# A gated linear attention and a SiLU feed-forward block on one core: weight conversion regrouped, GpSimd's arithmetic moved, activation tables shared, and the order of all engines written out

## The chip, the core and the metric

The kernel runs on one core of a Trainium2 chip. A core has five engines that run side by side, each through its own instructions in order: TensorE (PE in the profile; its weight loads are shown apart as PEld), VectorE (DVE), ScalarE (ACT), GpSimd (POOL) and SyncE (SP), which only starts transfers. The metric is the time of one execution in microseconds on the device. Three runs of the kernel before gave 823.57, 825.14 and 825.61 us, median 825.14.

## The reference

For each of 4 batches and 8 heads (768 steps, head size 48) a complex state is carried along the sequence and read out; the result goes through a feed-forward block with SiLU:

```python
scale = np.minimum(mag, 0.999) / (mag + 1e-06)          # mag = |a_re + i a_im|
a_re_n, a_im_n = (a_re * scale, a_im * scale)
for t in range(S):
    new_re = ar * S_re - ai * S_im
    new_im = ar * S_im + ai * S_re
    kv = np.einsum('bhd,bhe->bhde', k[:, :, t], v[:, :, t])
    S_re, S_im = (new_re + kv, new_im)
    y[:, :, t] = np.einsum('bhd,bhde->bhe', q[:, :, t], S_re)
...
h = x @ w_in                                            # x: 3072 x 384, w_in: 384 x 2048
g = h * (1.0 / (1.0 + np.exp(-h)))
return (g @ w_out).astype(np.float32)                   # w_out: 2048 x 384
```

q, k, v and the gates are float32. The two weight matrices arrive as float64.

## The kernel before

The sequence is cut into chunks of 128 steps. A block n is one chunk of one batch with all 8 heads: 24 blocks, taken as 12 pairs p. Per pair the work is:

- **Gates.** `gates_log` (lines 203 to 235) and `gates_angle` (237 to 250) turn a_re and a_im into the logarithm of the capped magnitude (tile `l`) and the angle in turns (tile `th`), both 128 x 768 for a pair. ACT does squares, Ln, Exp and arctangent, DVE and POOL the arithmetic between them: POOL adds and multiplies `mag` (L227, L231).
- **Phases and sums.** `phases` (264) and `sums` (285) are matmuls with a triangle of ones, which make running sums of `th` and `l` over the chunk. `carried` (255) adds the last angle of the block one chunk earlier, by a transfer of one row and an addition on POOL (L262).
- **Rotation.** `trig` (279) takes sine and cosine, `decays` (297) the exponentials of the running sums, `rotated` (309) multiplies k and q by both (on POOL, L314, and DVE, L318), `turned` (322) transposes them: for blocks 0 to 3 (`EARLY`) on PE with a copy by ACT, later by DVE in pieces of 32 x 32 (L339) and 12 transfers (L344).
- **Attention.** `weights` (347) makes q times k and masks it (L356), `state` (391) updates the carried state (L404, and L405 on POOL), `output` (359) makes the attention's result, already transposed, as tile `xT`, the feed-forward's input. A third of its rows goes through a small tile `y3` and six transfers (L389).
- **Feed-forward.** `hidden` (411) makes 256 of the 2048 hidden columns for a pair (6 matmuls 128 x 256), a tanh on ACT and one operation on DVE (L420); `result` (424) multiplies them into the output, 4 matmuls 128 x 384. A pair has 8 of each; I call one such piece an h group or an r group.

The weights are converted from float64 once, as they arrive, by `load_w` (125 to 156), in 28 units: 12 of w1 (128 x 512) and 16 of w2 (128 x 384). Each unit is loaded as pairs of 32-bit words; ACT squares the upper word (L143), DVE joins the words in five operations (L144 to L152), and a sixth (L154) sets weights under the float32 range to zero, with the square as the test. An h or r group of pair 0 or 1 cannot run before the units it reads.

The program has a set-up part (lines 569 to 657), in which pairs 0 and 1 go through the feed-forward beside the conversion and pairs 0 to 2 through the attention, and ten steps p = 3 to 12 (`step`, 461), which run the feed-forward of pair p - 1, the attention of pair p and the gates of pairs p + 1 and p + 2. Only PE's order is that of the program text (`manual_schedule` with PE alone); the order on the other engines is chosen by a scheduler at build time, except that table loads and table functions on ACT are chained in text order. ACT must load a table (L186) when it changes between groups of functions.

A last part checks the smallest decay, and only if it is too small would a slow form of the whole computation (`step_by_step`) run; with these inputs it does not.

Of the kernel before, what the change touches and what calls it, by code (L numbers as in the profile page):

```python
# [17 lines left out]
LN_CAP = math.log(0.999)  # L18
# [9 lines left out]
L_MIN = -60.0  # L28


@with_exitstack
def kernel(
# [36 lines left out]
    EARLY = 4  # L69
# [6 lines left out]
    moe = fast.enter_context(tc.tile_pool(name="moe", bufs=2))  # L76
    p_m = fast.enter_context(tc.tile_pool(name="p_m", bufs=2, space=PSUM))
    p_h = fast.enter_context(tc.tile_pool(name="p_h", bufs=2, space=PSUM))
    p_o = fast.enter_context(tc.tile_pool(name="p_o", bufs=4, space=PSUM))
# [12 lines left out]


    def load_a(p):
        for name, ap in (("re", a_re), ("im", a_im)):
            A[p][name] = pre.tile([C, 2, H, D], F32, tag=name, name=f"{name}{p}", bufs=2)
            for i in range(2):
                b, c = place(2 * p + i)
                nc.sync.dma_start(
                    out=A[p][name][:, i], in_=ap[b].rearrange("h (c p) d -> p c h d", p=C)[:, c])  # L100

    def load_x(n, queue=None):
        b, c = place(n)
        for name, ap in (("k", k), ("q", q), ("v", v)):
            X[n][name] = ld.tile([C, H, D], F32, tag=name, name=f"{name}{n}",
                                 bufs=4 if name == "v" else 2)
            (queue or nc.sync).dma_start(
                out=X[n][name], in_=ap[b].rearrange("h (c p) d -> p c h d", p=C)[:, c])

    w1 = consts.tile([C, ND, DF], F32)  # L110
    w2 = consts.tile([C, NJ, DM], F32)

    def load_w1(cols, dc):


        last = (H - 2) * D
        third = D // ND
        rows = [(0, 2 * dc * D, D), (D, last + third * dc, third),
                (64, (2 * dc + 1) * D, D), (64 + D, last + D + third * dc, third)]
        load_w(w1[:, dc, ts(cols, WC)], [(at, w_in[r:r + n, ts(cols, WC)]) for at, r, n in rows])  # L120
# [4 lines left out]
    def load_w(dst, parts):  # L125

# [5 lines left out]
        raw = moe.tile([C, WC, 2], I32, tag="raw", name="raw", bufs=3)[:, 0:n]  # L134
        for at, src in parts:
# [3 lines left out]
        t = dst.bitcast(I32)  # L139
        u = moe.tile([C, WC], I32, tag="wu", name="u", bufs=1)[:, 0:n]  # L140
        x = moe.tile([C, WC], F32, tag="wx", name="x", bufs=1)[:, 0:n]

        nc.scalar.activation(out=x, in_=hi.bitcast(F32), func=AF.Square)  # L143
        nc.vector.tensor_scalar(out=t, in0=hi, scalar1=3, scalar2=0x3FFFFFF8,  # L144
                                op0=ALU.logical_shift_left, op1=ALU.bitwise_and)
        nc.vector.scalar_tensor_tensor(out=t, in0=hi, scalar=-0x40000000, in1=t,
                                       op0=ALU.bitwise_and, op1=ALU.bitwise_or)
        nc.vector.tensor_scalar(out=u, in0=t, scalar1=-0x800000, scalar2=None,
                                op0=ALU.bitwise_and)
        nc.vector.scalar_tensor_tensor(out=u.bitcast(F32), in0=lo, scalar=2.0 ** -52,  # L150
                                       in1=u.bitcast(F32), op0=ALU.mult, op1=ALU.mult)
        nc.vector.tensor_tensor(out=dst, in0=dst, in1=u.bitcast(F32), op=ALU.add)  # L152

        nc.vector.scalar_tensor_tensor(out=dst, in0=x, scalar=1.265625 * 2.0 ** -30, in1=dst, op0=ALU.is_ge,  # L154
                                       op1=ALU.mult)
# [10 lines left out]

    one_b = consts.tile([C, 1], F32)
    nc.gpsimd.memset(one_b, 1.0)
    half_pi_b = consts.tile([C, 1], F32)
    nc.gpsimd.memset(half_pi_b, math.pi / 2)  # L170
    ident = consts.tile([C, C], F32)
# [5 lines left out]
    chained = []  # L177

    def chain(ins):
        if chained:  # L180
# [4 lines left out]
    def table(name):  # L185
        chain(nc.scalar.preload_act_table_set(name))  # L186
# [5 lines left out]
    def flat(t):  # L192
# [612 lines left out]
```

## Time and profile before

| | |
|---|---|
| median of three runs | 825.14 us |
| the profiled execution | 825.82 us |
| its span, first to last instruction | 824.0 us |
| mean granted clock of TensorE | 0.92 |
| DVE busy | 430.0 us (52%) |
| ACT busy | 300.4 us (36%) |
| POOL busy | 131.8 us (16%) |

The page of the profile gives the busy time of each engine, the same in 40 equal slices of the span, the costliest groups of instructions with the idle time before them and what ended it, and the chain of work that ended last. The trace can also be asked for the busy time in any stretch, for the instructions of an engine in order of time, and for what each engine waited for. A group's row reads: line, engine, operation, output <- inputs, shape, count | busy us, mean ns of one | idle us before, and what ended it. The granted clock is the share of TensorE's full speed that it was allowed.

### The profile page before, as it was taken

The numbers are of one execution on the slowest core, as the hardware profiler recorded it, in microseconds if no ns is written. First come the engines' busy times: TensorE is split into PE (matmuls) and PEld (weight loads), VectorE is DVE, ScalarE is ACT, GpSimd is POOL, SyncE is SP. The second block draws the span as 40 slices with busy tenths as digits, with TensorE's granted clock in tenths as the row PEclk, the third lists the DMA queues.
The fourth block names the chain that finished last, engine by engine and source line by source line (L and its number), as shares of the span: only waits on it lengthen the run. The fifth ranks groups of instructions, "written<-read, shape, count | busy, mean of one in ns | idle before, by whom it ended". The sixth has DMA issues, their size and how long they took to land.

```text
span 824.0 us, 9608 instructions
## 1 busy us (share of the span) xinstructions
PE 701.7 (85%) x3488; PEld 524.2 (64%) x3488; DVE 430.0 (52%) x622; ACT 300.4 (36%) x470; POOL 131.8 (16%) x108
## 2 busy tenths in 40 slices
PE   0586468908896599999999999899999899999997
PEld 0365345605574486777777877677768677777774
DVE  2858858796556635653663565526436613521110
ACT  4655522451135441541543624515515411411111
POOL 0020210140005103230240231121212400200000
PEclk9768779867897699999999999899999899999999
DMA  9613645425513533524415434434344142230000
GB/s 175 118 39 85 121 126 115 96 65 127 96 30 73 91 54 54 114 34 89 78 20 102 76 48 85 76 43 88 62 77 79 25 86 49 31 68 9 20 0 24
DMA packets 281943, 58.68 MB, mean 71 GB/s; under 512 B 274056, under 2 KB 278304, under 8 KB 281888
## 3 DMA queue, kind: packets, MB, share of 16 engines
q1 hardware_dynamic: 275648, 56.80, 37.4%
q10 hardware_dynamic: 6240, 1.18, 1.1%
q8 instruction: 30, 0.49, 0.2%
q14 instruction: 25, 0.20, 0.1%
HBM read 36.25 MB, written 4.76 MB: 50 GB/s over the span
## 4 chain that ended last, share of the span: by engine, by line
PE 60%; DVE 13%; issue 12%; ACT 7%; DMA 2%; POOL 2%; SPq 2%; ACTq 1%; DVEq 0%; POOLq 0%
PE o L430 25%; PE h L416 23%; PE a L352 3%; PE y L372 2%; PE s L399 2%; PE y L375 2%; DVE sq L339 2%; ACT L186 2%; PE L L291 2%; ACT mag L189 1%; DVE qr L318 1%; PE phase L270 1%; ACT cs L189 1%; POOL mag L227 1%; DMA raw<-in_moe_w_in_dram 1%
## 5 line engine op out<-in xcount | busy, mean ns | idle before, releaser
L430 PE MATMUL o<-w,g 128*128 128x384 f32 x768 | 275.5, 507 | 48.0 <-DVE w L154 47.3
L416 PE MATMUL h<-xT,w 128*128 128x256 f32 x1152 | 271.5, 387 | 3.9 <-DMA xT<-y 2.3
L416 PEld LDWEIGHTS h<-xT,w 128*128 128x128 f32 x1152 | 221.7, 194 | 55.9 <-issue 7.9
L430 PEld LDWEIGHTS o<-w,g 128*128 128x128 f32 x768 | 148.7, 197 | 143.5 <-DVE w L154 54.1
L420 DVE SCALAR_TENSOR_TENSOR g<-g,h 128x512 f32<-128x512 f32 x96 | 65.5, 682 | 276.3 <-ACT g L189 276.0
L189 ACT ACTIVATE g<-h 128x512 f32<-128x512 f32 x96 | 57.2, 597 | 312.9 <-PE h L416 312.9
L352 PE MATMUL a<-T 96*128 96x128 f32 x384 | 52.1, 292 | 14.3 <-DMA T<-sq 9.1
L352 PEld LDWEIGHTS a<-T 96*128 96x128 f32 x384 | 50.5, 207 | 18.3 <-DVE re L245 9.5
L186 ACT ACT_TABLE_LOAD x45 | 57.7, 1283 | 10.5 <-issue 9.7
L405 POOL TENSOR_TENSOR S<-S,decs 96x384 f32<-96x384 f32 x16 | 14.8, 925 | 238.3 <-DVE S L404 211.4
L227 POOL TENSOR_TENSOR mag<-mag,s 128x768 f32<-128x768 f32 x11 | 26.0, 2363 | 153.9 <-DVE s L199 108.5
L318 DVE TENSOR_TENSOR kr<-L,cs 128x768 f32<-128x768 f32 x24 | 41.9, 1769 | 14.4 <-POOL L L314 14.3
L270 PE MATMUL phase<-th,upto 128*128 128x384 f32 x48 | 21.4, 572 | 27.9 <-DVE th L249 23.2
L372 PE MATMUL y<-w,v 128*64 128x128 f32 (+1 forms) x384 | 42.6, 300 | 1.4 <-DVE w L356 1.2
L314 POOL TENSOR_TENSOR L<-k,L 128x384 f32<-128x384 f32 x20 | 20.9, 1061 | 129.6 <-ACT L L189 102.0
L399 PEld LDWEIGHTS s<-v,kr 128*96 128x96 f32 x320 | 33.4, 182 | 11.3 <-DVE w L356 7.4
L399 PE MATMUL s<-v,kr 128*96 128x48 f32 x320 | 33.8, 264 | 6.0 <-DVE w L356 6.0
L189 ACT ACTIVATE mag<-mag 128x768 f32<-128x768 f32 (+1 forms) x39 | 30.5, 789 | 23.1 <-POOL mag L227 21.0
L356 DVE TENSOR_TENSOR w<-a,upto 128x512 f32<-128x512 f32 x48 | 31.7, 683 | 12.9 <-PE a L352 12.8
L375 PE MATMUL y<-T,S 96*64 96x128 f32 x320 | 36.3, 287 | 0.0
L143 ACT ACTIVATE x<-raw 128x384 f32<-128x384 f32 (+1 forms) x28 | 17.0, 606 | 48.8 <-DVE w L154 45.0
L381 ACT COPY xT<-y 128x384 f32<-128x384 f32 x24 | 11.4, 473 | 57.6 <-PE y L375 39.3
(63 smaller groups left out, 641.6 us busy)
## 6 DMA issues: line engine op xcount, KB each, us to landing
T<-sq SPq DMA_DIRECT2D x240, 64.0 KB
raw<-in_moe_w_out_dram SPq DMA_DIRECT2D x16, 384.0 KB
re<-in_a_re_dram SPq DMA_DIRECT2D x24, 192.0 KB
im<-in_a_im_dram SPq DMA_DIRECT2D x24, 192.0 KB
raw<-in_moe_w_in_dram SPq DMA_DIRECT2D x24, 192.0 KB
out_dram<-ot SPq DMA_DIRECT2D x24, 192.0 KB
v<-in_v_dram SPq DMA_DIRECT2D x22, 192.0 KB
k<-in_k_dram SPq DMA_DIRECT2D x22, 192.0 KB
```

The lines of the kernel that those rows point to most:

```text
L186: chain(nc.scalar.preload_act_table_set(name))
L189: chain(nc.scalar.activation(out=out, in_=in_, func=func, **kw))
L227: lambda s1=s1, mag=mag: helper.tensor_tensor(out=mag, in0=mag, in1=s1, op=ALU.add),
L318: nc.vector.tensor_tensor(out=x[w + "r"], in0=heads(e).unsqueeze(2).to_broadcast([C, H, 2, D]), in1=x["cs"], op=ALU.mult)
L352: nc.tensor.matmul(ps[:, h], lhsT=x["kT"][:, hh * HH + h], rhs=x["qT"][:, hh * HH + h], start=True, stop=True)
L356: nc.vector.tensor_tensor(out=x["w", hh], in0=ps, in1=upto.unsqueeze(1).to_broadcast([C, HH, C]), op=ALU.mult)
L372: nc.tensor.matmul(to, lhsT=v_[:, cols], rhs=x["w", h // HH][:, h % HH], start=True, stop=not carried)
L375: nc.tensor.matmul(to, lhsT=x["S"].rearrange("p h d -> p (h d)")[:, cols], rhs=x["qT"][:, h], start=False, stop=True)
L399: nc.tensor.matmul(ps[:, h], lhsT=x["kr"][:, h].rearrange("p c d -> p (c d)"), rhs=x["v"][:, h], start=True, stop=True)
L416: nc.tensor.matmul(ps[:, ji], lhsT=w1[:, dc, ts(jp * 2 + ji, C)], rhs=A[p]["xT"][:, dc], start=(dc == 0), stop=(dc == ND - 1))
L420: nc.vector.scalar_tensor_tensor(out=g, in0=g, scalar=1.0, in1=ps, op0=ALU.add, op1=ALU.mult)
L430: nc.tensor.matmul(A[p]["o"][m], lhsT=A[p]["g", jp][:, ji, ts(m, C)], rhs=w2[:, j], start=(j == 0), stop=(j == NJ - 1))
```

## The change

- **Conversion.** The sixth operation per unit (L154) is gone. ACT does two passes per unit in place of one: a square scaled up, and a Relu whose sum goes to a column of a new tile `tiny`, which is above zero only if some weight is under the float32 range. The last check then also looks at `tiny`, and the slow form, which would convert again with the mask, runs in that case too. The units are ordered in four rounds of 3 units of w1 and 4 of w2; each round feeds two h and two r groups of both pairs, which PE takes together. Five buffers for arriving words in place of three.
- **GpSimd.** None of its arithmetic is left: `mag`, `rotated`, `state` and `carried` do it on DVE. In its place POOL starts transfers: in the set-up the loads of a_re, a_im of pairs 1 to 4, of q, k, v of pairs 1 to 3, and the six transfers of `y3`; throughout, those of `decs`. The results leave through ACT's queue (L479 after).
- **Gates.** Absolute values move from DVE to ACT; the factor 0.5 of `l` goes into the matrix of ones (`half`), which saves DVE an operation per pair.
- **Tables.** Tanh is taken from the table that also has arctangent or sine, so there are three loads in a step of the loop.
- **Transposes.** Blocks 4 to 7 are also transposed on PE (`EARLY = 8`), through the two buffers of `p_m`.
- **Order.** In the ten steps every engine's order is that of the text, and the text is a list of names (`usual`, and `first` for p = 3). The PSUM space of the set-up is given to a third buffer for h and one for phases and sums; the squares of a pair's gates are made a step earlier.

```diff
-    EARLY = 4
+    EARLY = 8
...
-        raw = moe.tile([C, WC, 2], I32, tag="raw", name="raw", bufs=3)[:, 0:n]
+        raw = su.tile([C, WC, 2], I32, tag="raw", name="raw", bufs=5)[:, 0:n]
...
-        nc.scalar.activation(out=x, in_=hi.bitcast(F32), func=AF.Square)
...
-        nc.vector.scalar_tensor_tensor(out=dst, in0=x, scalar=1.265625 * 2.0 ** -30, in1=dst, op0=ALU.is_ge,
-                                       op1=ALU.mult)
+        joined(nc, dst, lo, hi, u)
+        x = su.tile([C, WC], F32, tag="wx", name="x", bufs=1)[:, 0:n]
+        nc.scalar.activation(out=x, in_=hi.bitcast(F32), func=AF.Square, scale=2.0 ** 15)
+        nc.scalar.activation(out=x, in_=x, func=AF.Relu, scale=-1.0, bias=least_b,
+                             accum_out=tiny[:, ds(len(units), 1)])
...
-            (nc.vector if n < EARLY else nc.gpsimd).tensor_tensor(
+            nc.vector.tensor_tensor(
                 out=e, in0=x[w].rearrange("p h d -> p (h d)"), in1=e, op=ALU.mult)
...
-                nc.sync.dma_start(out=xT[64 * r + D:64 * r + 64, dc],
-                                  in_=y3[64 * r + third * dc:64 * r + third * (dc + 1)])
+                (nc.sync if late else nc.gpsimd).dma_start(
+                    out=xT[64 * r + D:64 * r + 64, dc],
+                    in_=y3[64 * r + third * dc:64 * r + third * (dc + 1)])
...
-            nc.gpsimd.tensor_tensor(out=new, in0=new, in1=by, op=ALU.mult)
+            nc.vector.tensor_tensor(out=new, in0=new, in1=by, op=ALU.mult)
...
-        ps = p_h.tile([C, 2, T], F32, tag="h", name=f"h{p}_{jp}")
+        pool = late[2] if late and jp % 3 == 2 else p_h
+        ps = pool.tile([C, 2, T], F32, tag="h", name=f"h{p}_{jp}")
...
-    conv = [(1, s, lambda s=s, dc=dc: load_w1(s, dc)) for s in range(2) for dc in range(ND)]
+    conv = []
     for s in range(4):
+        conv += [(1, s, lambda s=s, dc=dc: load_w1(s, dc)) for dc in range(ND)]
         conv += [(2, j // 2, lambda j=j: load_w2(j)) for j in range(4 * s, 4 * s + 4)]
-        if s < 2:
-            conv += [(1, s + 2, lambda s=s, dc=dc: load_w1(s + 2, dc)) for dc in range(ND)]
...
+        groups("r0 r0 r1 r1 h1 h1")
...
+    usual = ("c h h E kA qA L F h kB h tA G r qB r h tB r th h A X r h r aA pA sA yA h pB aB S r lA "
+             "sB yB r lB D r")
+    first = ("c h h E kA qA L F h kB h G r qB r h th r tA h A tB X r h r aA pA sA yA h pB aB S r lA "
+             "sB yB r lB D r")
+    by_hand.append(True)
+    with tc.manual_schedule():
         for p in range(3, NP + 1):
-            step(p, parts(hidden, p - 1), parts(result, p - 1))
+            step(p, parts(hidden, p - 1), parts(result, p - 1), first if p == 3 else usual)
```

In the list h and r are groups of the feed-forward; E are the decays, k, q and t the rotation and transposes of a block, a, s and y its weights, state and output, p and l its phases and sums, S sine and cosine, L, F, G, th and D parts of the gates, c, A and X loads; A and B behind a letter name the two blocks of the pair.

Three places of the order. The first is VectorE in the set-up, before; `raw` is an arriving unit, `w_79` is w1 and `w_80` w2, `u` and `x` the two helper tiles, `g` the result of a tanh.

```order
L144 TENSOR_SCALAR w_79<-raw 128x512
L146 SCALAR_TENSOR_TENSOR w_79<-raw,w_79 128x512
L148 TENSOR_SCALAR u<-w_79 128x512
L150 SCALAR_TENSOR_TENSOR u<-raw,u 128x512
L152 TENSOR_TENSOR w_79<-w_79,u 128x512
L154 SCALAR_TENSOR_TENSOR w_79<-x,w_79 128x512
L420 SCALAR_TENSOR_TENSOR g_0_793<-g_0_793,h_0_786 128x512
```

The same engine in the set-up of the change, where w1 is `w_84`:

```order
L45 TENSOR_SCALAR w_84<-raw 128x512
L47 SCALAR_TENSOR_TENSOR w_84<-raw,w_84 128x512
L49 TENSOR_SCALAR u<-w_84 128x512
L50 SCALAR_TENSOR_TENSOR u<-raw,u 128x512
L52 TENSOR_TENSOR w_84<-w_84,u 128x512
L462 SCALAR_TENSOR_TENSOR g_2_798<-g_2_798,h_2_791 128x512
```

The multiplication by the mask, which came last and waited for ACT's square, is gone; the unit is ready one operation earlier.

The second place is TensorE in the set-up, before, from the sums of pair 2 on; `xT_369` and `xT_584` are the inputs of pairs 0 and 1, `o_0_694` and `o_0_816` their outputs.

```order
L291 MATMUL L_868<-l_704,upto 128x384
L416 MATMUL h_2_897<-xT_584,w_79 128x256 x6
L430 MATMUL o_0_694<-w_80,g_2_779 128x384 x2
L430 MATMUL o_1_695<-w_80,g_2_779 128x384 x2
L416 MATMUL h_3_922<-xT_584,w_79 128x256 x6
L430 MATMUL o_0_694<-w_80,g_3_813 128x384 x2
L430 MATMUL o_1_695<-w_80,g_3_813 128x384 x2
L430 MATMUL o_0_816<-w_80,g_2_904 128x384 x2
L430 MATMUL o_1_817<-w_80,g_2_904 128x384 x2
L416 MATMUL h_4_1048<-xT_369,w_79 128x256 x6
```

TensorE at the same place of the change; here pairs 0 and 1 have `xT_385` and `xT_649`, and pair 2's angles are `th_835`.

```order
L457 MATMUL h_2_956<-xT_649,w_84 128x256 x6
L457 MATMUL h_3_966<-xT_649,w_84 128x256 x6
L457 MATMUL h_4_986<-xT_385,w_84 128x256 x6
L457 MATMUL h_5_996<-xT_385,w_84 128x256 x6
L306 MATMUL phase_1006<-th_835,upto 128x384
L306 MATMUL phase_1011<-th_835,upto 128x384
L327 MATMUL L_1016<-l_834,half 128x384
L327 MATMUL L_1020<-l_834,half 128x384
L472 MATMUL o_0_946<-w_85,g_2_963 128x384 x2
L472 MATMUL o_1_947<-w_85,g_2_963 128x384 x2
```

Groups now come in twos per pair, and the r groups stand further behind the h groups whose results they read, and behind the conversions.

The third place is GpSimd in the set-up, before, after its constants: its work on pairs 1 to 3.

```order
L227 TENSOR_TENSOR mag_267<-mag_267,s_265 128x768
L231 TENSOR_TENSOR mag_267<-mag_267,im_115 128x768
L227 TENSOR_TENSOR mag_703<-mag_703,s_701 128x768
L231 TENSOR_TENSOR mag_703<-mag_703,im_292 128x768
L262 TENSOR_TENSOR th_720<-th_720,carry_725 1x384
L262 TENSOR_TENSOR th_720<-th_720,carry_728 1x384
L227 TENSOR_TENSOR mag_989<-mag_989,s_987 128x768
L231 TENSOR_TENSOR mag_989<-mag_989,im_735 128x768
```

GpSimd of the change, the end of the loads that stand ahead of the first of the six transfers of `y3` (`y_0_387`) into pair 0's `xT_385`:

```order
L145 DMA v_344<-in_v_dram 128x8x48
L134 DMA im_1025<-in_a_im_dram 128x8x48
L134 DMA im_1025<-in_a_im_dram 128x8x48
L145 DMA v_557<-in_v_dram 128x8x48
L134 DMA re_1024<-in_a_re_dram 128x8x48
L134 DMA re_1024<-in_a_re_dram 128x8x48
L145 DMA v_563<-in_v_dram 128x8x48
L428 DMA xT_385<-y_0_387 16x256
```

The engine's arithmetic is replaced by transfers that it starts, 24 of them ahead of the one that the first h group needs.

More of the change, by code (lines that the diff above doesn't have):

```diff
@@ L565, in turns, with groups @@
         both(trig, p)
-        table("exp_and_others")
+        table("exp")
         both(decays, p)
+    def groups(order):
+        for x in order.split():
+            (h if x[0] == "h" else r)(int(x[1]))
+    g = nc.gpsimd
     with tc.manual_schedule(engines={mybir.EngineType.PE}):
-        angles(0, True)
+        load_a(1, g)
+        gates(0, True)
+        table("trig")
+        gates_atan(0, True)
+        gates_square(1)
+        gates_angle(0, True)
         both(phases, 0)
@@ L629 @@
+        groups("r0 r0 h0 h0 r1 r1")
+        for n in (4, 5):
             turned(n)
[L630 to L648 removed]
+        groups("h1 h1")
+        gates(3)
+        attend(4)
+        attend(5)
+        table("atan")
```

472 lines of the change are left out of this document (238 added, 234 removed).

## The prediction

> **What bounds the kernel now.** I read the page first: the span, the busy time of each engine and the slices.
>
> ```profile
> span 824.0 us, 9608 instructions
> PE 701.7 (85%) x3488; PEld 524.2 (64%) x3488; DVE 430.0 (52%) x622; ACT 300.4 (36%) x470; POOL 131.8 (16%) x108
> PE   0586468908896599999999999899999899999997
> PEclk9768779867897699999999999899999899999999
> ```
>
> TensorE is full from slice 14 on and full of holes before. So I asked for the busy time in four stretches: to the first h group, from there to the first h group of pair 2 (the start of step 3), to the sums of step 3, and the rest.
>
> ```profile
> 0.00:66.00 66.00, 30.46 (x144) 22.93 (x145) 38.73 (x69) 35.17 (x59) 5.51 (x12) 0.77 0.68 109
> 66.00:250.80 184.80, 129.99 (x593) 91.72 (x591) 135.88 (x232) 66.21 (x104) 24.00 (x15) 0.83 0.44 95
> 250.80:292.40 41.60, 25.49 (x114) 18.84 (x114) 23.20 (x28) 20.36 (x29) 13.15 (x11) 0.71 0.47 83
> 292.40:818.20 525.80, 515.78 (x2641) 390.75 (x2639) 232.18 (x294) 178.19 (x279) 89.10 (x71) 0.99 0.33 57
> ```
>
> The columns are length, busy PE, PEld, DVE, ACT, POOL, granted clock, DMA share and GB/s. The last stretch is TensorE's: 515.8 of 525.8 us at clock 0.99. The second has 54.8 us of idle PE and a clock of 0.83, the third 16.1 idle at 0.71. What PE waited for there is in its groups and in time order:
>
> ```profile
> L430 PE MATMUL o<-w,g 128*128 128x384 f32 x768 | 275.5, 507 | 48.0 <-DVE w L154 47.3 <-DVE g L420 0.7
> 66.08 1.35 PE L416 MATMUL h<-xT,w 128*128 128x256 f32 x4
> 186.57 1.65 PE L430 MATMUL o<-w,g 128*128 128x384 f32 x2 [19.86 <-DVE w L154]
> 248.15 2.85 PE L430 MATMUL o<-w,g 128*128 128x384 f32 x8
> 253.25 4.93 PE L416 MATMUL h<-xT,w 128*128 128x256 f32 x12 [2.26 <-DMA xT<-y]
> 278.52 3.75 PE L352 MATMUL a<-T 96*128 96x128 f32 x16 [9.10 <-DMA T<-sq]
> ```
>
> In the second stretch r groups wait for converted weights, 47.3 us, the longest 19.86. In the third PE waits for transposes that come by transfer. After a wait the same matmuls run slower (4.93 us for an h group). What the pieces cost when PE is warm stands in the chain of waits:
>
> ```profile
> 292.43 1.29 PE L L291 x4
> 293.71 2.59 PE h L416 x12
> 296.31 2.58 PE o L430 x8
> 301.48 1.79 PE a L352 x16
> 305.84 1.32 PE s L399 x16
> 309.12 2.79 PE h L416 x12
> 347.82 1.29 PE L L291 x4
> 812.89 5.17 PE o L430 x16
> 75.88 1.05 PE L332 MATMUL tp<-ident,kr 128*96 128x128 f32 x8
> ```
>
> (The last row is from the timeline.) An h or r group is 2.59, a block's weights 1.79, its state 1.32, its output 1.96 (307.16 to 309.12), phases or sums of a pair 1.29, a block's transposes two rows of 1.05. A step of the loop is 347.82 - 292.43 = 55.4 us, and PE ends at 818.1.
>
> **The change part by part**, as a sum over the stretches.
>
> *To the first h group: 66 to 68.* The gates of pair 1 lose GpSimd:
>
> ```profile
> 46.72 2.55 POOL L227 TENSOR_TENSOR mag<-mag,s 128x768 f32<-128x768 f32 x1 [44.93 <-DMA raw<-in_moe_w_in_dram]
> 34.17 0.96 DVE L318 TENSOR_TENSOR kr<-L,cs 128x768 f32<-128x768 f32 x1
> 260.94 3.63 DVE L318 TENSOR_TENSOR kr<-L,cs 128x768 f32<-128x768 f32 x1 [2.11 <-POOL L L314]
> L318 DVE TENSOR_TENSOR kr<-L,cs 128x768 f32<-128x768 f32 x24 | 41.9, 1769 | 14.4 <-POOL L L314 14.3
> ```
>
> 2.55 on GpSimd becomes about 0.96 on DVE, the row of the same shape, and DVE's own operations lose the stretching beside GpSimd (3.63 for 0.96). But the six transfers of `y3` now stand in GpSimd's queue behind 24 others. What a transfer costs GpSimd to start, no row shows. The nearest rows are SP's starts of the same loads and of these six:
>
> ```profile
> L99 SPq DMA_DIRECT2D re<-in_a_re_dram x24: 367/613/2053, 0.8 to 577.6; - x24
> 59.16 3.76 SPq L389 DMA_DIRECT2D xT<-y  x6
> 95.18 4.59 POOL L227 TENSOR_TENSOR mag<-mag,s 128x768 f32<-128x768 f32 x1 [42.26 <-DVE s L199]
> ```
>
> SP needs 0.37 to 2.05 us. The far bound is GpSimd's own longest operation, 4.59. I take up to 2, near the row of the same transfer: 30 x 2 = 60 us fit ahead of the first h group, so it comes 2 us later at most. At the best it comes 6 us earlier (the pair's phases no longer wait for GpSimd). The Trainium skill (SBUF — State Buffer, section SBUF: two separate sides) says that the descriptors of a transfer started by GpSimd cannot be written while VectorE runs an operation that takes both ports, as tensor_scalar in SBUF may, and gives 3100 against 620 ns for one transfer so overlapped. No transfer is started by GpSimd in this trace; by that price 24 of them are an estimated 74 us, and the sum below would be some 25 us more.
>
> *From there to step 3: 184.8 to 141.* PE's work at full speed: 32 groups 82.8, attention of blocks 2 to 5 4 x 5.07 = 20.3, phases and sums of two pairs 5.2, transposes of blocks 2 and 3 4.2: 112.5. Added: transposes of blocks 4 and 5, 4.2, and as they go through two PSUM buffers, each emptied by a copy, some 4.4 more:
>
> ```profile
> L335 ACT COPY T<-tp 96x512 f32<-96x512 f32 x16 | 8.8, 582 | 6.0 <-PE tp L332 6.0
> L144 DVE TENSOR_SCALAR w<-raw 128x384 int32<-128x384 int32 (+1 forms) x28 | 13.7, 495 | 0.0
> L146 DVE SCALAR_TENSOR_TENSOR w<-raw,w 128x384 int32<-128x384 int32 (+1 forms) x28 | 18.5, 662 | 0.3
> L148 DVE TENSOR_SCALAR u<-w 128x384 int32<-128x384 int32 (+1 forms) x28 | 13.1, 469 | 0.3
> L150 DVE SCALAR_TENSOR_TENSOR u<-raw,u 128x384 f32<-128x384 uint32 (+1 forms) x28 | 17.9, 638 | 0.4
> L152 DVE TENSOR_TENSOR w<-w,u 128x384 f32<-128x384 f32 (+1 forms) x28 | 18.6, 664 | 0.5
> L154 DVE SCALAR_TENSOR_TENSOR w<-x,w 128x384 f32<-128x384 f32 (+1 forms) x28 | 18.4, 656 | 3.3 <-ACT x L143 1.8
> L143 ACT ACTIVATE x<-raw 128x384 f32<-128x384 f32 (+1 forms) x28 | 17.0, 606 | 48.8 <-DVE w L154 45.0 <-DMA raw<-in_moe_w_in_dram 3.9
> ```
>
> So PE is at 121. Do the weights keep up? A unit takes DVE the first five of these rows, 81.8 / 28 = 2.92 us, and loses 0.66 (18.4 in all, 17 of it here). DVE's 135.9 in this stretch become 135.9 - 17 - 3.8 (four transposes of 0.96 that PE takes) - 15 (five more units stand in its order ahead of the first tanh, eight in place of three) + 11 (GpSimd's 24.0 us at DVE's price: six operations of 0.96 and ten of about 0.55) = 111. Of 141 us that is 79%: DVE is no longer what ends last. A round of 7 units costs DVE 20 us and feeds eight groups, 20.7 us of PE, and PE has attention between the rounds. ACT's 66.2 gain a second pass, 23 units x 0.61 = 14, copies 8 x 0.58 = 5 and absolute values 4: 89. For waits that are left (y3 of pair 1 through GpSimd's queue 3, angles of pairs 2 and 3 that PE reaches before DVE 3, attention's two PSUM buffers 6) and a clock still below full (half of the 17.5 us that 130.0 of busy PE lie above 112.5) I add 20. Bounds: 121, if all is hidden, and 165, if ACT's in-order queue holds the rounds back.
>
> *Step 3 to its sums: 41.6 to 24.* The work is four h or r groups, phases, weights, state and output: 16.7. PE transposes blocks 6 and 7 itself, so the 9.10 and the slow clock behind it go; that costs 4.2 and about 2.8 for two buffers: 24.
>
> *The loop: 525.8 to 521.* The 10 us of idle PE go, most of them like this one, with half speed after it:
>
> ```profile
> 530.96 2.80 PE L399 MATMUL s<-v,kr 128*96 128x48 f32 x16 [2.90 <-DVE w L356]
> ```
>
> DVE had been stuck beside GpSimd; it now does all itself, about 30 us in a step of 55. With 3 us for the clock that is -13. New waits by the hand order: the third h group's result needs ACT to do a table load, four exponentials, seven passes of the gates and another load after the second tanh, some 11 us, while PE has five groups, 12.9; and `xT` of the next pair is complete only a transfer after the step's last output. I take 1 us per step, +8. Bounds: 0 and 5 per step, where the transfers of `xT` wait behind ten loads on SP.
>
> *End:* two scalings and a transfer after the last matmul, 5.9 as now. The mask's check adds small operations that run long before.
>
> Sum: 68 + 141 + 24 + 521 + 5.9 = 759.9, against 824.0 of span. The execution took 825.82, so 761.7; the runs' median lies 0.7 lower: **761**.
>
> **Rivals.**
> *GpSimd's queue is late (slower).* With P us to start a transfer, the first h group comes at 30 P + 2, and all behind it moves along. It decides from P = 2.2; at 3 the first h comes at 92 and the time is 785. From P = 4.4 on it is slower than before; at 4.59 it is 140, and 833. For it: 24 loads in order, each of small rows, some behind releases by DVE. Against: SP's rows for the same transfers, and GpSimd starts them tens of us ahead.
> *ACT bounds the set-up.* Its order mixes two passes per unit, copies and gates; if they hold the rounds, the second stretch is 165: 785. For it: L143 already waits 48.8 us. Against: those waits were for the mask operation that goes.
> *The hand order stalls in the loop.* One late transfer or tanh holds all behind it. At 5 us in each of nine steps: 761 - 8 + 45 = 798.
> *PE is dense at once.* 121 for the second stretch and no new waits: 761 - 20 - 8 = 733.
>
> **How the numbers follow.** The forecast, 745 to 780, gets 0.60; GpSimd's queue 0.16 (0.11 at about 785, 0.05 slower than before); ACT 0.10; stalls in the loop 0.07, of which 0.02 reach past 825; dense PE 0.07. The range goes from 732 to 806: dense PE at one end, the three slower cases short of 825 at the other. Within 0.3% is about what a measurement of this kernel can't tell from no change. Faster 0.92, same 0.01, slower 0.07.
>
> **What would show it.** Right: L154 gone from what PE waits for; the first h group near 68 and pair 2's first near 209; DVE's kr at 0.96; steps of 55 to 57 us; POOL's arithmetic absent. Wrong: PE waiting for `xT` with GpSimd's transfers before it; r groups still behind L52; ACT busy without gaps in the set-up; steps above 58.

## The result and the profile after

Four runs of the changed kernel gave 737.3 to 741.63 us, median **738.35**, against 825.38 for the kernel before: a ratio of 0.8956, 95% interval 0.8924 to 0.8988. The forecast was 761, its range 732 to 806. The page of the profile after, first the span and the busy times, then TensorE and its clock in 40 slices:

```profile
span 737.3 us, 9570 instructions
PE 678.7 (92%) x3552; PEld 513.2 (70%) x3552; DVE 392.2 (53%) x638; ACT 352.2 (48%) x589; POOL 72.1 (10%) x111
PE   0465999899999999999999999999999999999997
PEclk9986999999999999999999999999999999999999
```

TensorE is full from slice 4 on, where it was from slice 14 on. The busy time in three stretches, divided as before: to the first h group, to pair 2's first h group, to TensorE's last matmul (columns as in the prediction):

```profile
0.00:70.50 70.50, 27.93 (x144) 19.49 (x144) 50.51 (x95) 57.08 (x104) 28.25 (x46) 0.91 0.75 164
70.50:194.50 124.00, 119.37 (x620) 90.52 (x621) 86.93 (x168) 75.59 (x137) 21.29 (x30) 0.97 0.32 87
194.50:732.40 537.90, 531.45 (x2789) 403.20 (x2787) 254.80 (x377) 219.08 (x348) 22.55 (x36) 1.00 0.33 61
```

The third of these stretches in the kernel before, by the same view (there TensorE waits 2.26 us for `xT` ahead of pair 2's first h group, and the stretch begins ahead of that wait):

```profile
250.80:818.20 567.40, 541.27 (x2753) 409.59 (x2752) 255.38 (x322) 198.55 (x308) 102.24 (x82) 0.97 0.34 59
```

| stretch | before | forecast | after |
|---|---|---|---|
| to the first h group | 66 | 68 | 70.5 |
| from there to pair 2's first | 184.8 | 141 | 124.0 |
| from there to TensorE's end | 567.4 | 24 + 521 = 545 | 537.9 |
| end | 5.8 | 5.9 | 4.9 |
| span | 824.0 | 759.9 | 737.3 |

In the second stretch TensorE is idle for 4.6 us in place of 54.8, and its work takes 119.4 us in place of 130.0, at clock 0.97 for 0.83, although the transposes of blocks 4 and 5 were added. In the third it is idle for 6.4 us in place of 26.1. What TensorE still waits for (total, times, longest) shows no weights and hardly anything in the loop (first two and two later rows):

```profile
PE phase L306 <- DVE th L285: 25.2, 2, 22.9
PE h L457 <- DMA decs<-ends: 7.9, 1, 7.9
...
PE a L390 <- DMA T<-sq: 3.0, 5, 1.1
PE tp L370 <- ACT T L373: 2.6, 5, 1.7
```

The second row is the first h group of all: it waits for the transfers into its input `xT`, which GpSimd starts; the section on the first h group comes back to it.

Five steps of the loop, from pair to pair's first sums, take 55.1, 55.8, 55.1, 55.7 and 55.1 us (first and last row of the six):

```profile
246.37 0.81 PE L327 MATMUL L<-l,half 128*128 128x384 f32 x2
...
523.11 0.81 PE L327 MATMUL L<-l,half 128*128 128x384 f32 x2
```

### The profile page after: what moved, and what is told of

It reads as the page before. It is cut to its first block, busy times and chain, and to the rows that moved or that the text cites. A ratio compares the mean times of both kernels' runs of the same rounds, so it can differ in the third digit from the quotient of the medians.

```text
span 737.3 us, 9570 instructions
## 1 busy us (share of the span) xinstructions
PE 678.7 (92%) x3552; PEld 513.2 (70%) x3552; DVE 392.2 (53%) x638; ACT 352.2 (48%) x589; POOL 72.1 (10%) x111
## 4 chain that ended last, share of the span: by engine, by line
PE 64%; ACT 11%; DVE 9%; SPq 5%; issue 5%; DMA 4%; POOL 1%; DVEq 0%; ACTq 0%; POOLq 0%
PE o L472 23%; PE h L457 22%; PE a L390 5%; SPq L382 5%; PE s L439 4%; PE y L411 3%; ACT s L227 3%; ACT mag L227 2%; PE y L414 2%; PE L L327 2%; ACT L222 2%; DMA raw<-in_moe_w_in_dram 2%; DVE g L462 2%; PE phase L306 2%; DMA T<-sq 1%
## 5 line engine op out<-in xcount | busy, mean ns | idle before, releaser
L457 PE MATMUL h<-xT,w 128*128 128x256 f32 x1152 | 261.7, 382 | 7.9 <-DMA decs<-ends 7.9
L472 PE MATMUL o<-w,g 128*128 128x384 f32 x768 | 262.8, 490 | 0.0
L341 POOL DMA_DIRECT2D decs<-ends x48 | 30.1, 634 | 443.8 <-DMA ends<-eq 443.5
L390 PEld LDWEIGHTS a<-T 96*128 96x128 f32 x384 | 46.4, 194 | 14.1 <-issue 8.4
L390 PE MATMUL a<-T 96*128 96x128 f32 x384 | 48.3, 279 | 5.2 <-DMA T<-sq 3.0
L330 DVE TENSOR_SCALAR L<-L 128x384 f32<-128x384 f32 x24 | 13.3, 556 | 54.6 <-PE L L327 54.6
L395 DVE TENSOR_TENSOR w<-a,upto 128x512 f32<-128x512 f32 x48 | 32.0, 684 | 18.2 <-PE a L390 18.2
L478 ACT ACTIVATE ot<-o 128x384 f32<-128x384 f32 x24 | 11.8, 490 | 40.3 <-PE o L472 40.3
L439 PE MATMUL s<-v,kr 128*96 128x48 f32 x320 | 30.0, 247 | 0.9 <-DVE w L395 0.8
L227 ACT ACTIVATE s<-s 128x768 f32<-128x768 f32 (+1 forms) x39 | 30.5, 784 | 0.3
L306 PEld LDWEIGHTS phase<-th,upto 128*128 128x128 f32 x48 | 9.0, 207 | 28.6 <-issue 26.3
```

The lines of the kernel that those rows point to most:

```text
L227: chain(nc.scalar.activation(out=out, in_=in_, func=func, **kw))
L306: nc.tensor.matmul(ps, lhsT=upto, rhs=th, start=True, stop=True)
L390: nc.tensor.matmul(ps[:, h], lhsT=x["kT"][:, hh * HH + h], rhs=x["qT"][:, hh * HH + h], start=True, stop=True)
L395: nc.vector.tensor_tensor(out=x["w", hh], in0=ps, in1=upto.unsqueeze(1).to_broadcast([C, HH, C]), op=ALU.mult)
L439: nc.tensor.matmul(ps[:, h], lhsT=x["kr"][:, h].rearrange("p c d -> p (c d)"), rhs=x["v"][:, h], start=True, stop=True)
L457: nc.tensor.matmul(ps[:, ji], lhsT=w1[:, dc, ts(jp * 2 + ji, C)], rhs=A[p]["xT"][:, dc], start=(dc == 0), stop=(dc == ND - 1))
```

## The experiments

Twelve kernels: eight that undo parts of the change, two that do a part of it to the kernel before, one reordered, one meant to beat both. All stretches begin and end at the events of the table above. In five kernels (before, the two made from it, the two runs with the old order) TensorE waits for `xT` ahead of pair 2's first h group; there the third stretch begins ahead of that wait, 1.7 to 2.5 us before the group. The medians are of four or five runs, and each ratio is against runs of the kernel before made together with it.

| kernel | to first h | to pair 2's first h | to TensorE's end | median us |
|---|---|---|---|---|
| before | 66.0 | 184.8 | 567.4 | 825.38 |
| change | 70.5 | 124.0 | 537.9 | 738.35 |
| mask operation back | 65.0 | 124.7 | 537.6 | 733.96 |
| GpSimd arithmetic back | 72.4 | 127.9 | 533.1 | 741.14 |
| loop ordered by the scheduler | 68.1 | 122.6 | 566.4 | 763.39 |
| old order of units and groups | 67.9 | 127.8 | 539.5 | 740.71 |
| block 1's attention first | 62.0 | 129.2 | 537.5 | 736.06 |
| blocks 6, 7 by transfer | 69.2 | 122.6 | 545.0 | 744.02 |
| loads from SP | 61.5 | 129.5 | 537.6 | 736.32 |
| set-up's old parts together | 65.6 | 187.9 | 536.6 | 797.04 |
| the same, new order | 65.7 | 171.5 | 535.8 | 779.60 |
| before, no mask operation | 62.4 | 176.9 | 566.5 | 815.62 |
| before, no mask, no GpSimd | 61.6 | 165.7 | 560.5 | 798.94 |
| combined | 63.1 | 126.8 | 532.4 | 729.27 |

The set-up is the same in the change and in the run with the scheduler's loop, yet their first h groups lie 2.4 us apart. Differences of that size in the first column are not read.

### The mask operation, put back and taken away

```diff
-        nc.scalar.activation(out=x, in_=hi.bitcast(F32), func=AF.Square, scale=2.0 ** 15)
-        nc.scalar.activation(out=x, in_=x, func=AF.Relu, scale=-1.0, bias=least_b,
-                             accum_out=tiny[:, ds(len(units), 1)])
+        nc.scalar.activation(out=x, in_=hi.bitcast(F32), func=AF.Square)
+        nc.vector.scalar_tensor_tensor(out=dst, in0=x, scalar=1.265625 * 2.0 ** -30, in1=dst,
+                                       op0=ALU.is_ge, op1=ALU.mult)
```

> The changed kernel with the sixth operation per unit back on VectorE (and one pass on ScalarE in place of two). Theory A, slack: VectorE is busy 86.9 of 124.0 us between the first h group and pair 2's, so 17 us more of it still lie beside TensorE: 738 to 743 us, no h or r group waits for weights. Theory B, the mask operation and its wait on ScalarE's square made the 47 us of waits: r groups wait for weights again and the time is 755 us or more.

Measured: 733.96 us, ratio 0.8897 (0.8871 to 0.8922): some 4 us *faster* than the change, and below both theories. The busy times of the stretches with the mask operation back:

```profile
0.00:65.00 65.00, 24.85 (x144) 16.90 (x144) 49.15 (x93) 46.49 (x78) 25.55 (x43) 0.99 0.81 172
65.00:189.70 124.70, 118.26 (x621) 89.51 (x622) 102.56 (x198) 66.77 (x106) 23.27 (x33) 0.98 0.34 90
```

VectorE has 15.6 us more to do in the second stretch (102.56 for 86.93) and TensorE loses 0.7. What is gained lies ahead of the first h group (5.5 us, of which 2.4 may be chance by what is said above), where ScalarE is busy 46.5 of 65.0 us, in place of 57.1 of 70.5 with two passes per unit.

The other way round, the kernel before without the operation:

```diff
-        nc.scalar.activation(out=x, in_=hi.bitcast(F32), func=AF.Square)
...
-        nc.vector.scalar_tensor_tensor(out=dst, in0=x, scalar=1.265625 * 2.0 ** -30, in1=dst, op0=ALU.is_ge,
-                                       op1=ALU.mult)
```

> The kernel before without the sixth operation per unit and without ScalarE's square (weights under the float32 range are not set to zero). Theory A, VectorE was too full as a whole: the stretch from the first h group to pair 2's loses about the 17 us of the operation, 805 to 815 us. Theory B, the operation and its wait made the waits: that stretch falls from 185 to 145 us or less and the time to 790 us or less. Theory C, the order of conversions and groups made them: 818 us or more.

Measured: 815.62 us, ratio 0.9888 (0.9863 to 0.9913). Its second stretch, 7.9 us shorter than before, where theory A had 17:

```profile
62.40:239.30 176.90, 130.26 (x593) 90.80 (x591) 118.73 (x206) 52.49 (x79) 22.94 (x15) 0.85 0.46 100
```

What TensorE waits for there, from the view of waits:

```profile
PE o L426 <- DVE w L151: 41.2, 9, 15.2
```

The wait of 47.3 us for the mask operation's result became one of 41.2 for the result of the operation ahead of it. The operation was only where the wait was seen: theory B falls. The time lies between the bounds of theories A and C; whether the order made the wait, as C has it, is tried further down.

### GpSimd's arithmetic

```diff
-            nc.vector.tensor_tensor(
+            (nc.vector if n < 4 else nc.gpsimd).tensor_tensor(
                 out=e, in0=x[w].rearrange("p h d -> p (h d)"), in1=e, op=ALU.mult)
...
-            nc.vector.tensor_tensor(out=new, in0=new, in1=by, op=ALU.mult)
+            nc.gpsimd.tensor_tensor(out=new, in0=new, in1=by, op=ALU.mult)
...
-            nc.gpsimd.dma_start(out=decs[a * D:(a + 1) * D, n],
+            (nc.sync if late else nc.gpsimd).dma_start(out=decs[a * D:(a + 1) * D, n],
```

(and the same for `mag` and the carry).

> The changed kernel with the arithmetic of gates, rotation, state and carry back on GpSimd (and the loads of the decays back on SP in the loop). Theory A, sharing costs: VectorE's rotation goes from 0.96 to some 3 us beside GpSimd, the steps grow by 1 to 3 us each and the time is 750 to 765 us. Theory B, in the written order the rotation stands far enough ahead of its transposes: steps stay at 55 us and the time is 738 to 744 us.

Measured: 741.14 us, ratio 0.8981 (0.8947 to 0.9014). VectorE's kr, from the groups by line:

```profile
L354 DVE TENSOR_TENSOR kr<-L,cs 128x768 f32<-128x768 f32 x24 | 31.5, 1312 | 34.0 <-POOL L L350 33.9
```

The third stretch:

```profile
200.26:733.40 533.14, 530.65 (x2789) 403.00 (x2787) 227.89 (x295) 220.31 (x349) 99.12 (x82) 1.00 0.34 62
```

The operation is slower beside GpSimd, 1312 ns against a mean of 956 in the change, and VectorE waits 33.9 us for GpSimd; but the third stretch is 4.8 us *shorter*. In a written order that asks for the rotation early, GpSimd's share costs the loop nothing; theory B holds there. (The starts of `decs` went back to SP in the same run, so the 4.8 us are not the arithmetic's alone.) The second stretch pays 3.9 us.

To the kernel before, the mask operation being away already, the move to VectorE was worth more:

```diff
-            (nc.vector if n < EARLY else nc.gpsimd).tensor_tensor(
+            nc.vector.tensor_tensor(
...
-        helper = nc.vector if split else nc.gpsimd
+        helper = nc.vector
```

> The kernel before without the sixth operation per unit and without ScalarE's square (weights under the float32 range are not set to zero), and with GpSimd's arithmetic on VectorE. Theory A, operations that VectorE does slowly beside GpSimd made the units late: the stretch from the first h group to pair 2's falls to 150 us or less and the time to 785 us or less. Theory B, the units are late because VectorE's queue stands still in front of operations that wait, and the work comes too late together: the stretch stays at 165 us or more and the time at 800 us or more.

Measured: 798.94 us, ratio 0.9681 (0.9658 to 0.9703): 11.2 us off the second stretch and 6.0 off the third. The time is a little under theory B's bound and the stretch on its side; the wait for weights is still 32.5 us. In the third stretch TensorE's state waits for VectorE's weights (L352) as before the move; the views of its waits there have these rows, first without the mask operation alone, then with GpSimd's arithmetic moved too:

```profile
PE a L348 <- DMA T<-sq: 9.5, 1, 9.5
PE s L395 <- DVE w L352: 5.8, 2, 2.9
```

```profile
PE a L348 <- DMA T<-sq: 7.4, 1, 7.4
PE s L395 <- DVE w L352: 5.8, 2, 2.9
```

What got shorter lies in step 3: the wait for transposes, by 2.1 us, and that for the carried angle, 3.2 us in place of 4.7.

### The loop's order

```diff
-    by_hand.append(True)
-    with tc.manual_schedule():
+    with tc.manual_schedule(engines={mybir.EngineType.PE}):
```

> The changed kernel, where in the ten steps only TensorE's order is that of the text and the scheduler orders the other engines. Theory A, the written order is what keeps TensorE fed in the loop: steps of 57 us or more, 755 us or more. Theory B, the rest of the change frees the engines enough: steps of 55 to 56 us, 738 to 745 us.

Measured: 763.39 us, ratio 0.9258 (0.9228 to 0.9288). Theory A: the third stretch is 566.4 us, as long as before (567.4), though GpSimd does no arithmetic. TensorE's waits in total:

```profile
PE s L439 <- DVE w L395: 18.2, 9, 2.9
```

One of the nine in the order of time, on TensorE:

```profile
541.05 2.71 PE L439 MATMUL s<-v,kr 128*96 128x48 f32 x16 [2.92 <-DVE w L395]
```

and VectorE just before:

```profile
538.97 0.96 DVE L248 SCALAR_TENSOR_TENSOR s<-s,s 128x768 f32<-128x768 f32 x1 [4.09 <-ACT s L227]
540.31 1.28 DVE L395 TENSOR_TENSOR w<-a,upto 128x512 f32<-128x512 f32 x2
```

The weights of the second block (L395), which TensorE needs at once, stand on VectorE behind the sum of the next gates' squares (L248), and that waits 4.09 us for ScalarE. TensorE waits 2.92 us and then takes 2.71 us for a state that takes 1.48 when it has not waited. In the change's written order the two stand the other way round, as VectorE's timeline there shows:

```profile
298.98 1.28 DVE L395 TENSOR_TENSOR w<-a,upto 128x512 f32<-128x512 f32 x2
...
309.53 0.95 DVE L248 SCALAR_TENSOR_TENSOR s<-s,s 128x768 f32<-128x768 f32 x1
```

The kernel before had the same trouble with another operation: ahead of its wait of 2.90 us, which the prediction quotes, VectorE stood in front of the gates' angle, for ScalarE's arctangent (its timeline):

```profile
528.35 0.96 DVE L247 SCALAR_TENSOR_TENSOR mag<-re,mag 128x768 f32<-128x768 f32 x1 [3.31 <-ACT mag L189]
...
530.22 1.28 DVE L356 TENSOR_TENSOR w<-a,upto 128x512 f32<-128x512 f32 x2
```

### Transposes of blocks 6 and 7

```diff
-    EARLY = 8
+    EARLY = 6
```

> The changed kernel with blocks 6 and 7 transposed by VectorE and transfers, as before the change. By the prediction's terms step 3 saves TensorE 4.2 + 2.8 us of its own transposes and waits 9.1 us, as before, with half speed behind it: 738 to 748 us. Rival: in the written order the transposes are asked for early enough that the transfers are hidden: 731 to 736 us.

Measured: 744.02 us, ratio 0.9016 (0.8998 to 0.9033), as the prediction's terms had it. Step 3 waits for the transfers; from the waits of TensorE:

```profile
PE a L390 <- DMA T<-sq: 11.9, 7, 7.6
```

and the third stretch:

```profile
191.80:736.80 545.00, 532.38 (x2757) 404.19 (x2755) 258.30 (x381) 215.14 (x340) 22.61 (x36) 0.99 0.35 63
```

The third stretch grows by 7.1 us: TensorE is idle for 12.6 us in place of 6.4, and its work takes 0.9 us more, though it has two blocks less to transpose (4.2 us by the prediction's rows).

### What made the set-up dense

First the order alone: units converted, and h and r groups of pairs 0 and 1 taken, as before.

```diff
-    for s in range(4):
-        conv += [(1, s, lambda s=s, dc=dc: load_w1(s, dc)) for dc in range(ND)]
-        conv += [(2, j // 2, lambda j=j: load_w2(j)) for j in range(4 * s, 4 * s + 4)]
+    conv = [(1, s, lambda s=s, dc=dc: load_w1(s, dc)) for s in range(2) for dc in range(ND)]
+    for s in range(4):
+        conv += [(2, j // 2, lambda j=j: load_w2(j)) for j in range(4 * s, 4 * s + 4)]
+        if s < 2:
+            conv += [(1, s + 2, lambda s=s, dc=dc: load_w1(s + 2, dc)) for dc in range(ND)]
...
-        groups("h0 h0 h1 h1")
...
-        groups("r0 r0 r1 r1 h1 h1")
+        groups("h0 r0 h1 h1 h0 r1")
...
+        groups("h1 r0 h1 r0")
```

> The changed kernel with the units converted, and the h and r groups of pairs 0 and 1 taken, in the order of the kernel before (no mask operation, no GpSimd arithmetic, loop by hand). Theory A, the order made the waits for weights (without the mask operation alone they were still 41.2 us): TensorE waits 20 us or more for converted weights, the stretch from the first h group to pair 2's is 150 us or more and the time 762 us or more. Theory B, the lighter VectorE is enough in any order: that stretch stays under 135 us and the time under 750 us.

Measured: 740.71 us, ratio 0.897 (0.8952 to 0.8988), theory B: no wait for weights, 127.8 us in the stretch. So neither the mask operation, nor GpSimd, nor the order, undone alone, brings the waits back. Then all the set-up's old parts at once:

```diff
-    EARLY = 8
+    EARLY = 4
...
-        raw = su.tile([C, WC, 2], I32, tag="raw", name="raw", bufs=5)[:, 0:n]
+        raw = su.tile([C, WC, 2], I32, tag="raw", name="raw", bufs=3)[:, 0:n]
...
-        u = su.tile([C, WC], I32, tag="wu", name="u", bufs=2)[:, 0:n]
+        u = su.tile([C, WC], I32, tag="wu", name="u", bufs=1)[:, 0:n]
...
-    g = nc.gpsimd
+    g = nc.sync
```

(with the mask operation, GpSimd's arithmetic and the old order as above, and the transfers of `xT` and `decs` from SP).

> The changed kernel with the set-up's old parts all at once: old order of units and groups, mask operation on VectorE, GpSimd arithmetic, three buffers for arriving units and one helper tile, all transfers from SP, blocks 4 to 7 transposed by transfers; the loop stays in the written order. Theory A, each of these parts alone is covered by the others, and together they are the set-up's gain: the stretch from the first h group to pair 2's is 165 us or more, TensorE waits 25 us or more for converted weights, and the time is 775 us or more. Theory B, the gain comes from what is left (tables, squares a step earlier, text order that the scheduler follows): that stretch is 140 us or less, the time 755 us or less.

> The same old parts, but with the new order of units and of h and r groups. Theory A, the order is what keeps TensorE from waiting when conversion is slow: at least 20 us less than the run with the old order. Theory B, the order does not matter even then: within 6 us of it.

Measured: 797.04 us, ratio 0.965 (0.9626 to 0.9674), with the old order; 779.60, ratio 0.9444 (0.9423 to 0.9465), with the new. The first kernel's second stretch and its waits there:

```profile
65.60:253.50 187.90, 130.25 (x592) 92.94 (x592) 121.56 (x211) 68.87 (x109) 20.19 (x14) 0.82 0.39 90
```

```profile
PE o L472 <- DVE w L182: 52.3, 9, 15.2
```

The same two views of the second kernel:

```profile
65.70:237.20 171.50, 132.56 (x588) 99.15 (x589) 114.12 (x203) 64.14 (x100) 19.38 (x14) 0.80 0.40 95
```

```profile
PE a L390 <- DMA T<-sq: 18.7, 2, 14.2
PE h L457 <- DVE w L182: 12.7, 3, 7.7
```

The parts together bring back the whole stretch: 187.9 us, against 184.8 before, at clock 0.82 for 0.83 and with 130.3 us of TensorE's work for 130.0. By the medians they cost 58.7 us and the scheduler's order of the loop 25.0, each undone alone; the two make 83.7 of the 87.0 us that the change gained, as a sum and not as a run.

What a part is worth depends on what lies beside it. Undone in the change, the mask operation costs the second stretch 0.7 us, GpSimd's arithmetic 3.9 and the order 3.8; done where the rest is old, they give 7.9, 11.2 (behind the mask operation) and 16.4 (in the last two runs). In these two the new order leaves 12.7 us of waits for weights in place of 52.3, and transposes by transfer become the longest wait. All together cost 63.9 us, but that takes in the buffers, the transfers from SP and the transposes of blocks 4 and 5, and of these only the loads were put back by themselves (below). Whether the parts lean on one another or one of these weighs most stays open.

VectorE is not full in the stretch, 121.6 of 187.9 us. Its own waits there, with all old parts and then in the change (the longest row of each), say where it stands:

```profile
DVE g L462 <- ACT g L227: 49.0, 12, 6.6
```

```profile
DVE g L462 <- ACT g L227: 19.1, 8, 9.3
```

With the old parts it stands for 49.0 us in front of the operation behind a tanh, and what comes later in its queue, conversions too, stands with it. Ahead of TensorE's longest wait for weights (15.2 us, up to 101.6) VectorE stood so for 5.5 us, and then worked on conversions nearly without a pause until the wait ended. That all of the 52.3 us come about in this way is not shown.

### Where the first h group lost its time

```diff
         attend(0)
+        attend(1)
         both(phases, 1)
         both(sums, 1)
-        attend(1)
```

> The changed kernel with the attention of block 1 ahead of pair 1's phases and sums on TensorE. Theory A, that order made the first h group late (70.6 against 66.1 us before): first h at 63 to 65 us and a time of 731 to 734 us. Theory B, the transfers that GpSimd starts made it late: first h at 69 us or more, time 737 us or more. Theory C, the first h comes earlier but the converted weights do not follow: the gain is lost behind it, 736 us or more.

```diff
-    g = nc.gpsimd
+    g = nc.sync
```

> The changed kernel with the loads of the gates and of q, k, v in the set-up started by SP in place of GpSimd. Theory A, the loads that wait for free buffers would hold the weight loads behind them in SP's queue: 745 us or more. Theory B, the queue does not matter here, since SP starts a load in some 0.8 us and GpSimd in 0.88: 736 to 741 us.

Measured: 736.06 us, ratio 0.8923 (0.8902 to 0.8943), and 736.32, ratio 0.8946 (0.8911 to 0.898). Each brings the first h group to 62 us, and each loses most of it in the stretch behind (by the time, theory C of the first and theory B of the second, though the first h group did move with the queue): pair 2's first h group comes at 191 us in both, 194.5 in the change. Where it goes is seen in TensorE's waits after the first h group; in the first kernel:

```profile
PE tp L370 <- DVE qr L354: 2.7, 1, 2.7
PE phase L306 <- DVE th L293: 2.5, 1, 2.5
```

and in the second:

```profile
PE phase L306 <- DVE th L293: 5.7, 1, 5.7
```

TensorE reaches pair 1's rotation and pair 2's angles before VectorE has made them.

Why the reordered kernel is early shows in what the change itself waits for. TensorE's timeline there, and the six transfers with the time from start to landing:

```profile
61.63 1.09 PE L411 MATMUL y<-w,v 128*64 128x128 f32 x16
70.58 7.75 PE L457 MATMUL h<-xT,w 128*128 128x256 f32 x24 [7.86 <-DMA decs<-ends]
```

```profile
L428 POOL DMA_DIRECT2D xT<-y x6: 484/484/523, 63.9 to 66.3; - x6
DMA to landing us min/median/max: 2.7/4.4/5.1
```

TensorE makes block 1's output last and then has nothing to do until the pieces of `xT` have landed, 7.86 us (the view names `decs`, started behind them in the same queue from 66.8 us on). In the kernel before, pair 1's phases and sums lay over the same transfers (59.16 to 66.08 us in the prediction's rows), and with block 1's attention first they do again: the wait is 3.94 us.

### The gains put together

The mask operation on VectorE, block 1's attention first, pair 2's phases behind two more r groups, and GpSimd's arithmetic in the loop alone:

```diff
-            nc.vector.tensor_tensor(out=mag, in0=mag, in1=th, op=ALU.add)
+            (nc.gpsimd if late else nc.vector).tensor_tensor(out=mag, in0=mag, in1=th, op=ALU.add)
...
-        groups("h0 h0")
+        groups("h0 h0 r1 r1")
         both(phases, 2)
         both(sums, 2)
```

> The changed kernel with the mask operation on VectorE in place of ScalarE's second pass, the attention of block 1 ahead of pair 1's phases and sums, pair 2's phases behind two more r groups, and GpSimd's arithmetic back in the loop alone. Theory A, these gains add up: first h group at 60 to 63 us, loop 3 to 5 us shorter, 725 to 731 us. Theory B, what the set-up gains is lost behind it as in the run with block 1's attention first: 732 us or more.

Measured: **729.27 us**, ratio 0.8841 (0.8821 to 0.8862), faster than both kernels.

```profile
0.00:63.10 63.10, 25.42 (x144) 17.45 (x144) 49.05 (x97) 46.21 (x79) 24.65 (x42) 0.98 0.83 174
63.10:189.90 126.80, 118.04 (x620) 89.28 (x621) 102.06 (x195) 67.08 (x106) 24.46 (x34) 0.98 0.32 89
189.90:722.30 532.40, 530.93 (x2789) 402.99 (x2787) 228.01 (x295) 220.08 (x349) 99.19 (x82) 1.00 0.34 62
```

The time is theory A's; the first h group comes at 63.1 us and the third stretch is 5.5 us shorter, each just past its range. From pair 2's first h group on TensorE is idle for 1.5 us of 532.4. Most of the idle time that is left lies ahead of the first h group, 37.7 us, against 8.8 in the second stretch.

## Why the prediction was right, and where it was not

**The direction and the place were right.** L154 is gone from TensorE's waits, the idle time between the first h group and pair 2's went, step 3 no longer waits for transfers, VectorE's kr takes 0.96 us in every instance, GpSimd has no arithmetic, and the steps take 55.1 to 55.8 us, where 55 to 57 was forecast. The time lies in the range, but below the likeliest case's 745 to 780, and 5 us above the rival of a dense TensorE (733), which had been given a chance of 0.07. That rival came nearest to what happened, and the range holds the time because the rival had set its lower end.

**The term that was mis-sized** is the allowance of 20 us in the second stretch, for waits that are left and a clock below full. TensorE's own work had been put at 121 us and took 119.4; the waits were 4.6. So 17 of the 22.6 us of error in the span are there. The prediction had VectorE at 79% busy and still kept 12 us for waits and half of what the low clock had cost before. VectorE's work came out lower too, 86.9 us against 111 forecast, 70% of the stretch. The clock term was not a cost of its own here: with TensorE hardly waiting, the granted clock of the stretch was 0.97. ScalarE, a rival as the bound of the set-up, was busy for 75.6 us there where 89 was forecast, and TensorE waited 0.6 us for its copies.

**The loop's new waits**, 8 us, did not come: idle TensorE is 6.4 us over the whole third stretch, step 3 with it, and that stretch is 7.1 us shorter than forecast. The reason given for the old waits was wrong. "DVE had been stuck beside GpSimd" falls with three runs: with GpSimd's arithmetic back the loop is no longer than without; with the scheduler's order the waits are there without GpSimd; and in the kernel before, the quoted kind of wait stayed at 5.8 us when GpSimd's arithmetic was taken away. (The 6.0 us that the third stretch lost there come with shorter waits in step 3.) VectorE stood in its own queue, in front of an operation that waited for ScalarE. With the rest of the change in place, the written order is worth 28.5 us in the third stretch (566.4 against 537.9): 11.6 of them are idle time of TensorE (18.1 against 6.4) and 16.9 slower work (548.4 against 531.5).

**The reason for the waits for weights** was half right. The sum counted work that VectorE loses, and that is a way in which they go. But the quoted row, "48.0 <-DVE w L154", names the last operation of a chain and not its cause, as the kernel before without it showed. No one of the three parts that were tried both ways is enough alone (they gave 7.9, 11.2 and 16.4 us of 60.8), and none of them alone is needed; how the rest of the gain is shared is not shown.

**ScalarE's second pass was costed at nothing ahead of the first h group.** By the medians it costs some 4 us more than the mask operation, ahead of the first h group, where no h groups lie beside it; so this part of the change is a small loss beside the others. Which of its passes delays what was not tried. The bound of 68 us for the first h group was passed by 2.5 us, which is about as much as it varied between kernels with the same set-up.

**GpSimd's queue** as a rival did not come true at its price, but one sign of it did: TensorE waits 7.86 us for `xT`, with GpSimd's transfers before it. What its starts take (shortest, median and longest, in ns):

```profile
L145 POOL DMA_DIRECT2D k<-in_k_dram x6: 882/886/896, 34.2 to 158.0; - x6
```

GpSimd's timeline before the first h group, with the idle time before a start and what ended it:

```profile
63.03 0.88 POOL L145 DMA_DIRECT2D v<-in_v_dram  x1 [9.92 <-PE y L411]
63.91 2.92 POOL L428 DMA_DIRECT2D xT<-y  x6
```

A load takes 0.88 us to start, less than half of the bound of 2, and a piece of `xT` 0.49 (2.92 for six). The queue was empty for 9.92 us before the load that stands ahead of `xT`, and that load waited for TensorE's own output. So the wait for `xT` is the time of this load's start, six more and their landing, which lies open because of TensorE's order. But the loads are not free for the set-up: from SP, pair 0's angles reach TensorE at 19.5 us in place of 22.9 and the first h group at 61.5.

## What to carry to other kernels

An engine named as the last to release a wait may only be the end of a chain: ask what stood ahead in its queue, and test by taking the named operation away, before its removal is priced as the gain. Where a fast consumer is fed by several slow parts, undoing one of them tells what it costs beside the others, not what it gave; undo them together as well, and add each to the old kernel. And an in-order engine that serves a dense TensorE needs the operation that TensorE asks for next ahead of any that waits for a third engine.

## What the runs showed of the hardware that was not expected

Starting a transfer on GpSimd hardly varied: 18 loads of k, q and v took 0.88 to 1.20 us each, in a set-up where VectorE was busy 50.5 of 70.5 us ahead of the first h group and 86.9 of 124.0 behind it. The load at 63.03, quoted above with 0.88 us, began beside one of VectorE's tensor_scalar operations:

```profile
63.01 0.35 DVE L49 TENSOR_SCALAR u<-w 128x384 int32<-128x384 int32 x1
```

The price of 3100 ns that the prediction took from the Trainium skill (SBUF — State Buffer, section SBUF: two separate sides) is seen in no start here. The loads of that line landed 3.2 to 9.6 us after they were started, and how much of that is waiting for descriptors these runs can't tell.

Beside GpSimd's arithmetic VectorE's kr took up to 1.75 us in the changed kernel with that arithmetic back, and up to 4.48 in the kernel before: how much slower it gets differs with the order of the work. Which of GpSimd's operations it met in the slowest cases was not looked into.
